# First two token chunks convolved on TensorE by tap diagonals, and x loaded as fp32, cast on VectorE and transposed for the rest

## The chip, the core and the metric

The kernel runs on one core of one Trainium2 chip. The metric is the device time of one execution in microseconds (us). Engines are named as the profile names them: PE is TensorE's matmuls and PEld its weight loads, DVE is VectorE, ACT is ScalarE, POOL is GpSimd and SP is SyncE. A DMA is issued from the queue of an engine: here SP, POOL and, in the changed kernel, ACT.

## What is computed

A causal depthwise convolution over the sequence with 7 softmaxed taps per head (8 heads of 24 channels), followed by a two-layer network with a beta-swish between its layers, over 32768 tokens of 192 channels:

```python
def _attn_ref(x, weight):
    B, S, D = x.shape            # 8, 4096, 192
    H, K = weight.shape          # 8, 7
    w = softmax(weight, axis=-1)
    x_pad = np.concatenate([np.zeros((B, K - 1, D)), x], axis=1)
    idx = np.arange(S)[:, None] + np.arange(K)[None, :]
    x_unf = x_pad[:, idx, :].reshape(B, S, K, H, D // H)
    return np.einsum('hk,bskhg->bshg', w, x_unf).reshape(B, S, D)

def _moe_ref(x, w_in, w_out, beta):          # w_in 192 x 2048, w_out 2048 x 192
    h = x @ w_in
    g = h * (1.0 / (1.0 + np.exp(-beta * h)))
    return (g @ w_out).astype(np.float32)
```

## The kernel before

**Two streams.** The 32768 tokens are split into two streams s = 0 and 1 of 16384 tokens each, which are worked on together. With channels on partitions, one stream's 64 channels of a group lie on partitions 0 to 63 and the other stream's on 64 to 127; the 192 channels make NK = 3 such groups (kk). So each matmul of the first layer (line 257) contracts over 64 rows, and the two streams use the two halves of the array side by side. For that, both halves of `w_in_s` hold the same weights.

**Steps.** `steps` (line 61) lists stretches of tokens: 128, 128, 256, then 31 of 512 tokens, 34 steps in all. In step i, for each of 16 units u (a block of 128 hidden channels), `mm1(i, u)` makes six matmuls into a tile `ph` (three groups, two streams) and ACT turns it into `g` with Silu scaled by beta (line 259). Between the units, `mm2(i - 1, ...)` multiplies the hidden values of the step before with `w_out_s` into tiles `po` (line 293); `mm2_plan` says in which unit. When a pair of token blocks is complete, `store` copies `po` to `o_sb` on DVE (line 301) and SP writes it out (line 307). `ph` and `po` have two buffers each. For a step of 512 tokens the pairs complete in units 5, 7, 13 and 15, for one of 256 in units 11 and 15.

**The convolution.** Also between the units, DVE convolves the next step's tokens: `conv_ops(i + 1)` gives 22 entries, a beginning (which copies the last six columns of the chunk before into `xt`, line 220) and 21 taps, tap 0 a TENSOR_SCALAR (line 229), the others SCALAR_TENSOR_TENSOR (line 231), for each of three groups. They read the transposed x in `xt`, add in `acc` and end in `xc`, which mm1 of the next step reads. Two entries are issued after each unit.

**Fetching x.** A chunk j is 512 tokens of each stream. POOL loads it with eight DMAs that cast fp32 to bf16 on the way (line 96, tile `x_bf`, three buffers), and SP transposes it with four DMA transposes of 128 tokens into `xt` (line 104, three buffers). At the beginning of step i, ahead of its units, chunk j + 2 is transposed and chunk j + 3 is loaded, where j is the chunk of step i; step i + 1 then convolves chunk j + 2.

**The start.** The first 128 tokens are convolved on PE: DVE makes seven copies of `x0` weighted with the taps (line 168), and 42 matmuls with a shifted identity (line 185) add them up, with the channels on partitions; ACT evicts them to `xc` (line 190). w_in comes in five POOL DMAs (line 80) and three copies inside the chip from one half to the other (line 84). w_out comes in four SP DMAs (line 142), and POOL scales it by 1/beta into `w_out_s` (line 207, 16 instructions). Everything passes through `pin`, which keeps the order of the program on each engine and queue.

Of the kernel before, what the change touches and what calls it, by code (L numbers as in the profile page):

```python
# [10 lines left out]
FP32 = mybir.dt.float32  # L11
BF16 = mybir.dt.bfloat16
# [6 lines left out]
def kernel(  # L19
# [14 lines left out]
    group = D // H  # L34
# [3 lines left out]
    NK = D // 64  # L38
    NS = 2
    TS = B * S // NS  # L40
    TILE = 512

# [8 lines left out]
    xbf_pool = ctx.enter_context(tc.tile_pool(name="xbf", bufs=3))  # L51
# [8 lines left out]

    steps = [(0, 128), (128, 128), (256, 256)]
    steps += [(t, TILE) for t in range(TILE, TS, TILE)]
    n_steps = len(steps)


    x0 = consts.tile([128, NS, D], FP32, name="x0")
    pin(nc.sync.dma_start(out=x0, in_=xs[:, 0:128, :].rearrange("s p d -> p s d")))
    wbc = consts.tile([128, H, K], FP32, name="wbc")
    pin(nc.sync.dma_start(out=wbc, in_=weight.rearrange("h k -> (h k)").partition_broadcast(128)))
    beta16 = consts.tile([NF, 128], FP32, name="beta16")  # L70
    pin(nc.sync.dma_start(out=beta16, in_=moe_beta.rearrange("(c p) -> c p", p=128)))

    w_in_s = consts.tile([128, NK, F], BF16, name="w_in_s")
    w_in_v = moe_w_in.rearrange("(k c) f -> c k f", c=64)
# [4 lines left out]
    def load_w_in(half, f0, f1):  # L79
        pin(nc.gpsimd.dma_start(out=w_in_s[64 * half:64 * half + 64, :, f0:f1], in_=w_in_v[:, :, f0:f1]))  # L80

    def copy_w_in(half, f0, f1):
        o = 1 - half
        pin(nc.sync.dma_start(out=w_in_s[64 * o:64 * o + 64, :, f0:f1],
                              in_=w_in_s[64 * half:64 * half + 64, :, f0:f1]))

    xbf_of, xt_of = {}, {}

    def load_x(j, b0=0, b1=4):
        if j not in xbf_of:  # L90
            xbf_of[j] = xbf_pool.tile([128, 4, NK, NS, 64], BF16, name="x_bf")
        t = xbf_of[j]
        for b in range(b0, b1):
            for s in range(NS):
                src = xs[s, TILE * j + 128 * b:TILE * j + 128 * (b + 1), :]
                pin(nc.gpsimd.dma_start(out=t[:, b, :, s, :],  # L96
                                        in_=src.rearrange("p (k c) -> p k c", c=64)))

    def transpose_x(j, b0=0, b1=4):
        if j not in xt_of:  # L100
            xt_of[j] = xt_pool.tile([128, NK, LEAD + TILE], BF16, name="xt")
        for b in range(b0, b1):
            c = LEAD + 128 * b
            pin(nc.sync.dma_start_transpose(
                out=xt_of[j][:, :, c:c + 128],
                in_=xbf_of[j][:, b, :, :, :].rearrange("p k s c -> p (k s c)")))

# [7 lines left out]


    load_w_in(0, 0, 512)
    load_w_in(1, 0, 512)
    shift = consts.tile([128, 128 + PAD], BF16, name="shift")
    pin(nc.gpsimd.memset(shift, 0.0))  # L120
    pin(nc.gpsimd.affine_select(out=shift, in_=shift, compare_op=ALU.not_equal, fill=1.0,
                                base=PAD, pattern=[[-1, 128 + PAD]], channel_multiplier=1))
    id16 = consts.tile([NF, NF], FP32, name="id16")
    pin(nc.gpsimd.memset(id16, 0.0))
    pin(nc.gpsimd.affine_select(out=id16, in_=id16, compare_op=ALU.not_equal, fill=1.0,
                                base=0, pattern=[[-1, NF]], channel_multiplier=1))
    load_x(0, 0, 4)
    mask = consts.tile([128, NK, H], FP32, name="mask")
    pin(nc.gpsimd.memset(mask, 1.0))
    for s in range(NS):  # L130
        m = mask[64 * s:64 * s + 64, :, :]
        pin(nc.gpsimd.affine_select(out=m, in_=m, compare_op=ALU.is_ge, fill=0.0, base=0,  # L132
                                    pattern=[[64, NK], [-group, H]], channel_multiplier=1))
        pin(nc.gpsimd.affine_select(out=m, in_=m, compare_op=ALU.is_ge, fill=0.0, base=group - 1,  # L134
                                    pattern=[[-64, NK], [group, H]], channel_multiplier=-1))
    load_w_in(0, 512, 1024)
    load_w_in(1, 1024, 1536)
    load_w_in(0, 1536, 2048)
    load_x(1)

    for c in range(0, NF, 4):
        pin(nc.sync.dma_start(out=w_out_f[:, c:c + 4, :], in_=w_out_v[:, c:c + 4, :]))  # L142
        if c == 0:
            transpose_x(0, 0, 2)
            copy_w_in(0, 512, 1024)
        if c == 4:
            copy_w_in(1, 1024, 1536)
            transpose_x(0, 2, 4)
        if c == 8:
            copy_w_in(0, 1536, 2048)  # L150


    mx = consts.tile([128, H], FP32, name="mx")
    pin(nc.vector.tensor_reduce(out=mx, in_=wbc, axis=AX.X, op=ALU.max))
    pin(nc.vector.tensor_tensor(wbc, wbc, mx[:, :, None].to_broadcast([128, H, K]), ALU.subtract))
    pin(nc.scalar.activation(wbc, wbc, AF.Exp))
    pin(nc.scalar.activation(scrap, one, AF.Silu))
    sm = consts.tile([128, H], FP32, name="sm")
    pin(nc.vector.tensor_reduce(out=sm, in_=wbc, axis=AX.X, op=ALU.add))
    rs = consts.tile([128, H], FP32, name="rs")  # L160
    pin(nc.vector.reciprocal(rs, sm))
    taps = consts.tile([128, H, K], FP32, name="taps")
    pin(nc.vector.tensor_tensor(taps, wbc, rs[:, :, None].to_broadcast([128, H, K]), ALU.mult))


    xw = consts.tile([128, K, NS, D], BF16, name="xw")
    for k in range(K):
        pin(nc.vector.tensor_tensor(  # L168
            xw[:, k, :, :].rearrange("p s (h c) -> p s h c", c=group),
            x0.rearrange("p s (h c) -> p s h c", c=group),  # L170
            taps[:, None, :, k:k + 1].to_broadcast([128, NS, H, group]),
            ALU.mult))

    warm = psum_h.tile([128, 2, TILE], FP32, name="ph")
    for i in range(8):
        pin(nc.tensor.matmul(warm[:, i % 2, :], zeros[:, 0:128], zeros, start=True, stop=True))  # L176
    bps = psum_h.tile([128, 2, TILE], FP32, name="ph")
    pin(nc.tensor.transpose(bps[:, 0, 0:NF], beta16, id16))
    cva = psum_o.tile([128, 2, TILE], FP32, name="po")
    cvb = psum_o.tile([128, 2, TILE], FP32, name="po")  # L180
    cv = [cva[:, 0, 0:128], cva[:, 1, 0:128], cvb[:, 0, 0:128]]
    for k in range(K):
        for kk in range(NK):
            for s in range(NS):
                pin(nc.tensor.matmul(cv[kk][64 * s:64 * s + 64, :], xw[:, k, s, 64 * kk:64 * kk + 64],  # L185
                                     shift[:, k:k + 128], start=(k == 0), stop=(k == K - 1)))
    xc_of = {}
    xc_of[0] = xc_pool.tile([128, NK, TILE], BF16, name="xc")
    for kk in range(NK):
        pin(nc.scalar.activation(xc_of[0][:, kk, 0:128], cv[kk], AF.Copy))  # L190

    beta = consts.tile([128, NF], FP32, name="beta")
    pin(nc.vector.tensor_copy(beta, bps[:, 0, 0:NF]))
    rbeta = consts.tile([128, NF], FP32, name="rbeta")
    pin(nc.vector.reciprocal(rbeta, beta))

    tmp3 = consts.tile([128, NK, K, H], FP32, name="tmp3")
    for kk in range(NK):
        pin(nc.vector.tensor_tensor(tmp3[:, kk, :, :],
                                    mask[:, kk:kk + 1, :].to_broadcast([128, K, H]),  # L200
                                    taps.rearrange("p h k -> p k h"), ALU.mult))
    taps3 = consts.tile([128, NK, K], FP32, name="taps3")
    pin(nc.vector.tensor_reduce(out=taps3, in_=tmp3, axis=AX.X, op=ALU.add))


    for c in range(NF):
        pin(nc.gpsimd.tensor_scalar_mul(w_out_s[:, c, :], w_out_f[:, c, :], rbeta[:, c:c + 1]))  # L207


    def conv_ops(i):  # L210
        t0, n = steps[i]
        j, c0 = t0 // TILE, t0 % TILE
        ops = []

        def halo():
            xt = xt_of[j]
            if t0 % S == 0 or t0 == 128:
                pin(nc.vector.memset(xt[:, :, LEAD - PAD:LEAD], 0.0))
            elif c0 == 0:
                pin(nc.vector.tensor_copy(xt[:, :, LEAD - PAD:LEAD], xt_of[j - 1][:, :, TILE + LEAD - PAD:]))  # L220

        def tap(kk, k):
            xt, xc = xt_of[j], xc_of[i]
            acc = accs[i]
            src = xt[:, kk, LEAD - PAD + c0 + k:LEAD - PAD + c0 + k + n]
            w = taps3[:, kk, k:k + 1]
            a = acc[:, kk, 0:n]
            if k == 0:
                pin(nc.vector.tensor_scalar_mul(a, src, w))  # L229
            else:  # L230
                pin(nc.vector.scalar_tensor_tensor(  # L231
                    out=xc[:, kk, 0:n] if k == K - 1 else a, in0=src, scalar=w, in1=a,
                    op0=ALU.mult, op1=ALU.add))
# [144 lines left out]
```

## Time and profile before

| | us |
|---|---|
| median of 3 runs (lowest to highest) | 714.59 (713.95 to 716.54) |
| the profiled execution's time | 712.91 |
| its span in the profile | 711.2 |
| L257 matmuls (mm1), 3264 of them, busy | 432.7 |
| L293 matmuls (mm2), 7936 of them, busy | 422.4 |
| L259 activations, 544, busy | 574.9 |
| L231 taps into acc, 495, busy | 326.7 |
| L301 store copies, 124, busy | 68.9 |
| first matmul of mm1 | 10.92 from the start |

All times in views of the profile are in us from the start of the span, and durations in us or, where marked, ns. In a timeline row the first number is the start, the second the length of the row (several like instructions are merged, with their number after an x), then engine, line, operation, what it writes <- what it reads with the shape of both, and in brackets how long the engine stood idle before and what ended that. "SPq" is SP's queue. Consecutive instructions of an engine overlap a little, so the distance from one start to the next is shorter than a duration. In a table of windows, the window is followed by its length, the busy time and (in brackets) the number of instructions of PE, PEld, DVE, ACT and POOL, the granted clock, the DMA engines' share and GB/s.

### The profile page before, as it was taken

To read this page: it belongs to the slowest core of one execution; us is meant where nothing else is said; L and a number is where in the kernel's file an instruction comes from. 1 tells how busy PE (TensorE), PEld (TensorE's weight loads), DVE (VectorE), ACT (ScalarE), POOL (GpSimd) and SP (SyncE) were. 2 spreads that over 40 slices of the span, in tenths; PEclk is the share of its full clock that TensorE was granted. 3 is DMA by queue.
4 is the path that set the end of the run, shared out by engine and by line. 5 is a ranking of instruction groups with operands and counts; after the bars stand their busy time and mean duration, and the time that the engine had idled before them with its cause. 6 is when DMAs were issued, how large, how long until landed. Compare 5 with 4: busy or idle time off the path is not lost.

```text
span 711.2 us, 25346 instructions
## 1 busy us (share of the span) xinstructions
PE 687.7 (97%) x11379; PEld 524.5 (74%) x11379; DVE 502.2 (71%) x877; ACT 578.8 (81%) x552; POOL 218.2 (31%) x290
## 2 busy tenths in 40 slices
PE   5589999999999999999999999999999999999998
PEld 2466777777777777777777777777777777777777
DVE  4779776677687667678667768766776876676702
ACT  3489888888888888888888888888888888888882
POOL 9997332223333113333212333321233330000000
PEclk9999999999999999999999999999999999999999
DMA  9999554455555445555445555544555553221012
GB/s 132 149 95 96 81 88 69 72 84 79 75 80 87 69 73 85 75 72 87 79 71 78 74 74 81 88 71 71 83 80 74 80 85 64 58 62 52 28 44 68
DMA packets 194861, 55.38 MB, mean 78 GB/s; under 512 B 158128, under 2 KB 194752, under 8 KB 194752
## 3 DMA queue, kind: packets, MB, share of 16 engines
q0 software_dynamic: 103440, 13.58, 30.6%
q1 hardware_dynamic: 91312, 40.17, 22.3%
q8 instruction: 89, 1.46, 0.9%
q14 instruction: 20, 0.16, 0.1%
HBM read 28.94 MB, written 25.17 MB: 76 GB/s over the span
## 4 chain that ended last, share of the span: by engine, by line
PE 93%; POOL 2%; DMA 2%; DVE 2%; issue 0%; ACT 0%; SPq 0%; DVEq 0%; POOLq 0%
PE ph L257 46%; PE po L293 46%; PE po L316 2%; DVE acc L231 1%; POOL x_bf L96 1%; DMA w_in_s<-w_in_s 1%; DMA x_bf<-in_x_dram 1%; POOL w_in_s L80 0%; ACT g L259 0%; DVE xc L231 0%; DVE acc L229 0%; SPq L142 0%; POOL mask L132 0%; POOL mask L134 0%; DVE o_sb L320 0%
## 5 line engine op out<-in xcount | busy, mean ns | idle before, releaser
L259 ACT ACTIVATE g<-ph,beta 128x1024 bf16<-128x1024 f32 (+2 forms) x544 | 574.9, 1064 | 111.8 <-PE ph L257 107.4
L257 PE MATMUL ph<-xc,w_in_s 64*128 64x512 bf16 (+2 forms) x3264 | 432.7, 367 | 17.0 <-DMA w_in_s<-w_in_s 9.4
L293 PEld LDWEIGHTS <-g 64*128 64x128 bf16 x7936 | 359.6, 94 | 101.5
L293 PE MATMUL po<-w_out_s,g 64*128 64x192 bf16 x7936 | 422.4, 243 | 0.0
L231 DVE SCALAR_TENSOR_TENSOR acc<-xt,taps,acc 128x512 f32<-128x512 bf16 (+2 forms) x495 | 326.7, 727 | 0.0
L96 POOL DMA_DIRECT2D x_bf<-in_x_dram x256 | 197.5, 774 | 366.7 <-DMA xt<-x_bf 349.4
L257 PEld LDWEIGHTS <-w_in_s 64*128 64x128 bf16 x3264 | 168.2, 96 | 74.6 <-DMA w_in_s<-w_in_s 10.5
L301 DVE COPY o_sb<-po 128x384 f32<-128x384 f32 x124 | 68.9, 556 | 183.5 <-PE po L293 183.5
L231 DVE SCALAR_TENSOR_TENSOR xc<-xt,taps,acc 128x512 bf16<-128x512 bf16 (+2 forms) x99 | 66.5, 727 | 0.0
L229 DVE TENSOR_SCALAR acc<-xt,taps 128x512 f32<-128x512 bf16 (+2 forms) x99 | 41.8, 481 | 9.2 <-DMA xt<-x_bf 8.1
L207 POOL TENSOR_SCALAR w_out_s<-w_out_f,rbeta 128x192 bf16<-128x192 f32 x16 | 15.6, 992 | 0.1
L316 PE MATMUL po<-w_out_s,g 128*128 128x192 bf16 x128 | 10.7, 246 | 0.0
L316 PEld LDWEIGHTS <-g 128*128 128x128 bf16 x128 | 10.5, 98 | 0.2 <-issue 0.2
L320 DVE COPY o_sb<-po 128x192 f32<-128x192 f32 x8 | 2.9, 358 | 7.6 <-PE po L316 7.6
L176 PE MATMUL ph<-zeros 128*128 128x512 bf16 x8 | 3.6, 631 | 1.2 <-DVE one L112 1.2
L220 DVE COPY xt<-xt 128x18 bf16<-128x18 bf16 x28 | 4.6, 166 | 0.0
L185 PE MATMUL po<-shift,xw 128*64 128x128 bf16 x42 | 3.3, 314 | 1.2 <-DVE xw L168 1.2
L185 PEld LDWEIGHTS <-xw 128*64 128x64 bf16 x42 | 2.0, 152 | 2.4 <-DVE xw L168 2.4
L80 POOL DMA_DIRECT2D w_in_s<-in_moe_w_in_dram x5 | 3.3, 665 | 0.8 <-POOLq L362 0.8
L168 DVE TENSOR_TENSOR xw<-x,taps 128x384 bf16<-128x384 f32 x7 | 3.4, 553 | 0.0
L176 PEld LDWEIGHTS <-zeros 128*128 128x128 bf16 x8 | 1.0, 140 | 2.9 <-issue 1.7
L190 ACT ACTIVATE xc<-po 128x128 bf16<-128x128 f32 x3 | 0.6, 278 | 3.1 <-PE po L185 3.1
(30 smaller groups left out, 8.8 us busy)
## 6 DMA issues: line engine op xcount, KB each, us to landing
out_dram<-o_sb SPq DMA_DIRECT2D x124, 192.0 KB, 2.3
x_bf<-in_x_dram POOLq DMA_DIRECT2D x256, 48.0 KB, 3.1
xt<-x_bf SPq DMA_TRANSPOSE x128, 2.3
w_out_f<-in_moe_w_out_dram SPq DMA_DIRECT2D x4, 384.0 KB, 6.7
w_in_s<-in_moe_w_in_dram POOLq DMA_DIRECT2D x5, 192.0 KB, 5.5
out_dram<-o_sb SPq DMA_DIRECT2D x8, 96.0 KB, 1.6
w_in_s<-w_in_s SPq DMA_DIRECT2D x3, 192.0 KB, 6.8
x<-in_x_dram SPq DMA_DIRECT2D x1, 192.0 KB, 2.6
```

The source lines that it names most:

```text
L96: pin(nc.gpsimd.dma_start(out=t[:, b, :, s, :], in_=src.rearrange("p (k c) -> p k c", c=64)))
L176: pin(nc.tensor.matmul(warm[:, i % 2, :], zeros[:, 0:128], zeros, start=True, stop=True))
L185: pin(nc.tensor.matmul(cv[kk][64 * s:64 * s + 64, :], xw[:, k, s, 64 * kk:64 * kk + 64], shift[:, k:k + 128], start=(k == 0), stop=(k == K ...
L207: pin(nc.gpsimd.tensor_scalar_mul(w_out_s[:, c, :], w_out_f[:, c, :], rbeta[:, c:c + 1]))
L220: pin(nc.vector.tensor_copy(xt[:, :, LEAD - PAD:LEAD], xt_of[j - 1][:, :, TILE + LEAD - PAD:]))
L229: pin(nc.vector.tensor_scalar_mul(a, src, w))
L231: pin(nc.vector.scalar_tensor_tensor(out=xc[:, kk, 0:n] if k == K - 1 else a, in0=src, scalar=w, in1=a, op0=ALU.mult, op1=ALU.add))
L257: pin(nc.tensor.matmul(ph[:, s, 0:n], w_in_s[r, kk, ts(fc, 128)], xc_of[i][r, kk, 0:n], start=(kk == 0), stop=(kk == NK - 1)))
L259: pin(nc.scalar.activation(g_of[i][:, fc, :, 0:n], ph[:, :, 0:n], AF.Silu, scale=beta[:, fc:fc + 1]))
L293: pin(nc.tensor.matmul(po[:, q, 0:D], g_of[i][r, fc, s, ts(b, 128)], w_out_s[r, fc, :], start=(phase == 0 and fc == 0), stop=(phase == 1 a ...
L301: pin(nc.vector.tensor_copy(o_sb, po[:, :, 0:D]))
L316: pin(nc.tensor.matmul(po[:, 0, 0:D], g_of[i][:, fc, s, ts(b, 128)], w_out_s[:, fc, :], start=(fc == 0), stop=(fc == NF - 1)))
```

## The change

*The layout of channels.* A channel c is now q * 3 + k: partition q of 64, group k of 3. All three groups of a partition belong to one head, so that one column of taps (`tapn`) serves all of them.

*The first two chunks of 128 tokens.* `x0` now holds 512 tokens as fp32. PE transposes the first two blocks (`transpose_0`, three fp32 transposes each); ACT and DVE copy them to `xr`, in which six zero columns lead. `diag` holds for each tap a diagonal matrix of the unnormalized taps, doubled over both column halves. `conv_0` makes for each tap and stream one matmul of 64 rows, 128 columns of weights and 3 x 128 moving columns, in fp32r; as the diagonal is doubled, the result has the channels on both halves of the partitions. `evac_0` multiplies it by 1/sum. Steps 0 and 1 therefore use another form of mm1: `mm1_pair(i, u)` computes hidden block u from the lower half and block u + 8 from the upper half, 256 moving columns (two streams of 128 tokens), so that each half of `w_in_s` needs only its own 1024 hidden channels at first. Four POOL loads bring these, and four copies inside the chip fill the rest, before step 2. The second pair of blocks of `x0` is transposed within step 0 and goes to `xt_of[0]`.

*The steps.* 128, 128, then five of 256, then 29 of 512: 36 steps. A convolution of 256 tokens takes one instruction per tap over all three groups.

*w_out.* Its four loads move from SP's queue to POOL's, behind w_in. Of the scalings, 12 go to DVE within step 0, 4 stay on POOL.

*Fetching x.* From chunk 2 on, SP loads a chunk in two fp32 DMAs (`xf`, two buffers), DVE casts it in two copies to `xbf` (two buffers), and SP transposes it. These three entries (`fetch`) are added to the end of the step's list of DVE work, after the convolution; the list is spread over the first 14 units.

```diff
-    steps += [(t, TILE) for t in range(TILE, TS, TILE)]
+    steps += [(t, 256) for t in range(TILE, 3 * TILE, 256)]
+    steps += [(t, TILE) for t in range(3 * TILE, TS, TILE)]
...
+    def load_x(j, s, b0=0, b1=NB, eng=None):
...
+        src = xs[s, TILE * j + 128 * b0:TILE * j + 128 * b1, :]
+        pin((eng or nc.sync).dma_start(out=xf_of[j][:, b0:b1, s, :],
+                                       in_=src.rearrange("(b p) d -> p b d", p=128)))
+    def cast_x(j, s, b0=0, b1=NB, eng=None):
...
+        pin((eng or nc.vector).tensor_copy(
+            xbf_of[j][:, b0:b1, :, s, :].rearrange("p b k q -> p k b q"),
+            xf_of[j][:, b0:b1, s, :].rearrange("p b (q k) -> p k b q", k=NK)))
...
+    HF = F // 2
+    for f in range(0, HF, 512):
+        for s in range(NS):
+            load_w_in(s, HF * s + f, HF * s + f + 512)
     for c in range(0, NF, 4):
-        pin(nc.sync.dma_start(out=w_out_f[:, c:c + 4, :], in_=w_out_v[:, c:c + 4, :]))
...
+        pin(nc.gpsimd.dma_start(out=w_out_f[:, c:c + 4, :], in_=w_out_v[:, c:c + 4, :]))
+    for b in (0, 2):
+        for s in range(NS):
+            load_x(1, s, b, b + 2, nc.gpsimd)
...
+    tap_ps = misc[:, 0, 0:K]
+    pin(nc.tensor.matmul(tap_ps, sel.rearrange("h s g j -> h (s g j)"), taps, start=True, stop=True))
...
+    for k in range(K):
+        pin(nc.vector.tensor_scalar_mul(diag[:, k, :, :], ident2, etap[:, k:k + 1]))
...
+    def transpose_0(po, b):
...
+        for kk in range(NK):
+            pin(nc.tensor.transpose(t[:, kk, :], v[:, kk, :], ident))
+        return t
+    def conv_0(cv, b, k0, k1):
+        for k in range(k0, k1):
+            for s in range(NS):
+                pin(nc.tensor.matmul(
+                    cv[:, s, 0:NK * 128], diag[half_of(s), k, :, :].rearrange("p s q -> p (s q)"),
+                    xr[half_of(s), :, 128 * b + k:128 * b + k + 128],
+                    start=(k == 0), stop=(k == K - 1)))
...
+    t0_ = transpose_0(po01, 0)
...
+    pin(nc.tensor.transpose(beta_ps, beta16, ident[0:NF, 0:NF]))
+    t1_ = transpose_0(po01, 1)
+    pin(nc.scalar.activation(xr[:, :, PAD:PAD + 128], t0_, AF.Copy))
...
+    conv_0(cv0, 0, 0, K)
...
+    evac_0(cv0, 0, 0, nc.scalar)
+    evac_0(cv0, 0, 1, nc.vector)
...
+    for f in range(0, HF, 512):
+        for s in range(NS):
+            copy_w_in(s, HF * s + f, HF * s + f + 512)
...
+        parts = [(kk, kk + 1) for kk in range(NK)] if n == TILE else [(0, NK)]
+        return [begin] + [lambda k=k, p=p: tap(k, *p) for k in range(K) for p in parts]
...
+    def mm1_pair(i, u):
+        ph = psum_h.tile([128, NS, TILE], FP32, name="ph")
+        fcs = (u, u + NF // 2)
+        for kk in range(NK):
+            for h in range(2):
+                pin(nc.tensor.matmul(ph[:, h, 0:256], w_in_s[half_of(h), kk, ts(fcs[h], 128)],
+                                     xc_of[i][half_of(h), kk, 0:256],
+                                     start=(kk == 0), stop=(kk == NK - 1)))
...
+    def fetch(j, eng=None):
+        ops = []
+        for s in range(NS):
+            ops.append(lambda s=s: cast_x(j, s, eng=eng))
+        def go():
+            for b in range(NB):
+                transpose_x(j, b)
+            if (j + 2) * TILE < TS:
+                for s in range(NS):
+                    load_x(j + 2, s)
+        ops.append(go)
+        return ops
+    def extra_ops(i):
+        if i < 3 or i == 4:
+            return []
+        j = {3: 2, 5: 3, 6: 4}.get(i, steps[i][0] // TILE + 2)
+        return fetch(j) if j * TILE < TS else []
...
+        if i == 0:
...
+            for u in range(NF // 2):
+                mm1_pair(0, u)
+                if u < 2:
...
+                elif u == 2:
+                    cv1 = psum_o.tile([128, 2, TILE], FP32, name="po")
+                    conv_0(cv1, 1, 0, 4)
+                elif u == 3:
+                    conv_0(cv1, 1, 4, K)
...
+                elif u > 4:
+                    for c in FC0[4 * u - 20:4 * u - 16]:
+                        scale_w_out(c, nc.vector)
+                    cv[u - 1]()
+            continue
...
-            if (j + 2) * TILE < TS:
-                transpose_x(j + 2)
-            if (j + 3) * TILE < TS:
-                load_x(j + 3)
+        dve = dve + extra_ops(i)
+        done = 0
         for u in range(NF):
             mm1(i, u)
             for t in plan[u]:
                 mm2(i - 1, *t)
-            for op in conv[:2]:
+            upto = len(dve) * (u + 1) // (NF - 2)
+            for op in dve[done:upto]:
                 op()
-            conv = conv[2:]
+            done = max(done, upto)
```

## The prediction

> **What bounds the kernel now.** I read the page first, then windows by stage, then the timeline of the engines that feed TensorE. The page and the stage table:
>
> ```profile
> PE 687.7 (97%) x11379; PEld 524.5 (74%) x11379; DVE 502.2 (71%) x877; ACT 578.8 (81%) x552; POOL 218.2 (31%) x290
> ...
> 11.00:31.00 20.00, 7.32 (x96) 4.75 (x96) 11.85 (x38) 6.37 (x17) 19.60 (x23) 1.00 1.46 175
> 31.00:39.70 8.70, 8.19 (x162) 7.01 (x160) 4.43 (x10) 7.20 (x18) 8.70 (x11) 1.00 0.41 32
> 39.70:52.50 12.80, 9.81 (x162) 7.89 (x159) 12.70 (x22) 10.49 (x17) 12.79 (x18) 1.00 1.83 111
> 52.50:69.20 16.70, 16.12 (x216) 10.41 (x218) 15.71 (x26) 14.85 (x15) 13.06 (x18) 1.00 1.01 87
> ```
>
> After the window come its length and the busy time of PE, PEld, DVE, ACT and POOL. Between 11 and 31 us PE works 7.3 us out of 20: the first step waits for halves of w_in to be copied (the group of L257 with 64x128 names 9.4 us of it). From 69.7 us on PE is never idle: the step for tokens 1024 begins at 69.70, the next at 90.62, so a full step lasts 20.92 us (16 units of 1.307). The last full step begins 28 steps after 90.62, at 676.4, and 34.8 us later the span of 711.2 ends. So a gain can only come from the first 70 us, while a loss can come anywhere that another engine is made to need over 20.92 us a step. DVE is the candidate, and it depends on the transposes of x. DVE's rows of the timeline around a step's start (320.7):
>
> ```profile
> 318.34 0.56 DVE L301 COPY o_sb<-po 128x384 f32<-128x384 f32 x1 [1.49 <-PE po L293]
> 320.96 0.56 DVE L301 COPY o_sb<-po 128x384 f32<-128x384 f32 x1 [2.06 <-PE po L293]
> 321.43 0.16 DVE L220 COPY xt<-xt 128x18 bf16<-128x18 bf16 x1
> 321.63 1.28 DVE L229 TENSOR_SCALAR acc<-xt,taps 128x512 f32<-128x512 bf16 x3
> ```
>
> The transposes, from SP's rows of the timeline in three other steps, and all of them by their line:
>
> ```profile
> 133.74 5.10 SPq L104 DMA_TRANSPOSE xt<-x_bf  x4
> ...
> 322.02 5.72 SPq L104 DMA_TRANSPOSE xt<-x_bf  x4
> ...
> 405.70 6.54 SPq L104 DMA_TRANSPOSE xt<-x_bf  x4
> ```
>
> ```profile
> L104 SPq DMA_TRANSPOSE xt<-x_bf x128: 1183/1197/2642, 9.5 to 639.7; - x128
> DMA to landing us min/median/max: 2.3/2.3/7.8
> ```
>
> In each step SP issues four transposes in 5.1 to 6.5 us; one takes 1.2 us to issue and lands 2.3 us after its start. From the first start to the last landing that is 5.10 - 1.2 + 2.3 = 6.2 us at best, 6.8 in the middle row, 7.6 in the longest. No DVE instruction waits for it now: the four go out at a step's start and are convolved one step later. The taps are not blocked either; here is one convolution of 512 tokens that ran through:
>
> ```profile
> 54.48 1.38 DVE L229 TENSOR_SCALAR acc<-xt,taps 128x512 f32<-128x512 bf16 x3
> 55.78 10.01 DVE L231 SCALAR_TENSOR_TENSOR acc<-xt,taps,acc 128x512 f32<-128x512 bf16 x15
> 65.71 2.06 DVE L231 SCALAR_TENSOR_TENSOR xc<-xt,taps,acc 128x512 bf16<-128x512 bf16 x3
> 67.70 0.54 DVE L301 COPY o_sb<-po 128x384 f32<-128x384 f32 x1
> ```
>
> From 54.48 to 67.70, **13.2 us for 21 taps**. A store copy takes 0.48 us from start to start (328.80 to 329.28).
>
> **The start.** Removed: DVE's 7 weighted copies of x0 (3.4 us), 42 bf16 matmuls (3.3 us), the mask and the shift matrix. Added: 5 selector and identity steps on POOL ahead of its loads (rows of 0.1 to 0.3 us, so loads issue from 2.3 us instead of 1.3), 12 fp32 transposes of x, 28 fp32r matmuls of 384 columns, 7 diagonals on DVE. PE's order puts beta and the second block of x0 ahead of the first convolution; beta landed at 5.7 us before (PE's wait at 5.83). After it three transposes, to about 7.0. Of fp32r matmuls there is no row: bf16 at this stage needs 3.60/8 = 0.45 us for 512 columns, so 0.34 us for 384; if two halves of the array overlap, seven pairs take 2.4 us, and if neither overlap nor the two-byte rate holds (twice the bytes, no pairing) four times that, 9.4. I take 2.4, by the L257 rows, whose 64-row halves do overlap. With the eviction (three ACT rows of 0.28 us before, now one wider one) the first step starts at 10.3 us, against 10.92.
>
> Steps 0 and 1 use each w_in load on the half where it landed, so the 20 us window loses its waits. Step 0 has 16 activations of 0.45 us (7.2) and, on PE between its units, transposes and the second convolution, 2.4 us by the same rows in which ACT gets nothing: some 9.5 us. Step 1: 16 activations, 7.5. Step 2 had 16 activations in 10.22 us: 10.3. Each new 256-step needs 16 x 0.655 on PE and 10.2 on ACT: 10.6. The w_out loads go from SP's queue to POOL's, behind w_in's, and 12 of 16 scalings from POOL (0.99 us each) to DVE; that can delay step 1 by up to 2 us, and is covered while step 0 lasts. The four copies of w_in wait on SP and must land by step 2, at 27.3 us; their 6.8 us to landing leave room. Starts: 10.3, 19.8, 27.3, 37.6, 48.2, 58.8, and **step 6 (tokens 1280) at 69.4**. Step 7 (1536) could then begin at 80.0 against 90.62 before: **10.6 us gained**, if DVE keeps up. What "loads each half once" saves is one of five loads from memory; four copies inside the chip replace three.
>
> **The fetch, which decides.** x is now loaded by SP as fp32, two DMAs per chunk instead of POOL's eight, and DVE casts it (two copies of 768 elements). No row shows this copy; the nearest are the first tap, 0.43 us for 512 elements, and the store copy, 0.48 for 384. 256 more elements at the first tap's rate give some 0.6, at the store copy's slope 0.95; a gain is excluded, as DVE had no such work. I take 0.6, by the nearer form (one source, both sides in SBUF).
>
> The order matters more. A step's list is now 22 convolution entries, then two casts and the transposes. So the transposes of chunk j+2 go out at the end of the step, and the next step's first tap, which reads all 512 columns, needs all four landed. **DVE stands idle for the transposes** in every step. Behind the waiting tap are the other 20 taps and the store copies, hence the po buffers that mm2 wants at unit 8. DVE's loop, from one convolution's end to the next: cast 0.6, store copy of unit 13 0.48, cast 0.6, four transposes 6.8 with 0.15 for the two hand-overs (0.03 from copy to SP at 329.36 to 329.39, and about 0.12 after a landing), taps 13.2, store copies of units 5 and 7 0.96. Together **22.8 us against PE's 20.92**. Halo and the store copy of unit 15 fit into the wait. Ends: 21.7 (casts 0.5, transposes 5.9, which is issue without a pause, 3 x 1.2 + 2.3) and 24.3 (casts 0.95, transposes 7.6).
>
> The first such wait is worse, as step 6 has 256 tokens and convolves 512. Step 5's casts come after the store copy of unit 11 and end at 58.8 + 9.9; the transposes have landed 6.95 later, at 75.65. Taps 13.2 and one copy 0.48: chunk 3 is ready at 89.3, so step 7 begins there and the whole gain of the start is spent. Then 21.85 and 22.3 us for the next two convolutions (fewer store copies) and 26 x 22.8 = 592.8: the last step starts at 726.3 + 0.2, and with the unchanged 34.8 the span is **761.2**. The profiled execution of before took 712.91 for its span of 711.2, so 762.9; its median over runs was 1.7 higher, so **764 us**.
>
> The Trainium skill, in "DMA: Bandwidth & Descriptors", section "Rules for kernel authors", says to issue a DMA early, compute, and wait for it late, which speaks against this order. The trace of before keeps to it, with no wait for a transpose after 26 us; by the rule alone the cost would be whatever of 6.8 us a step isn't covered.
>
> **Rivals.** *The loop fits under PE* (not slower): the transposes would have to be down in 20.92 - 16.0 = 4.9 us. For it: POOL's casting loads, 30.6% of the DMA engines' time on the page, are gone, and no row shows transposes without them. Against: the 5.9 us that issue and one landing take at the least. Then only step 6's long convolution (13.7 us, ready at about 84) costs, and a step 7 bound by ACT at 16.6, 27 full ones and 34.8 end at 700.2: **703.6 us**. *The loop fits, but the start is slow*: fp32r at 9.4 us instead of 2.4 for both convolutions, 14 us of which step 0's activations hide a part: about **712 us**, no change. *The loop binds and casts are slow as well*: 23.5 a step, 26 x 0.7 more: **783 us**.
>
> **How the numbers follow.** Loop binds with fast casts 0.68, with slow casts 0.18, hidden fetch 0.11, hidden fetch with a slow start 0.03. The forecast is the first's 764 us. Its own range follows from the ends of the loop, 26 x -1.1 and 26 x 1.5, and 3 us of the start: 732 to 806. The range of 8 in 10 is 732 to 804: it leaves out the hidden fetches below and a corner above. Faster than 0.5% (the least that a measurement here can tell from no change) 0.11, within 0.03, slower 0.86.
>
> **What would show it.** Right: DVE waits for the transposes in every full step, 5 to 7 us; full steps 22 to 24 us apart; PE idle near 2 us a step, for DVE's xc or its o_sb copies; PE's wait for copies of w_in in the first 31 us gone; step 6 starting near 70 us. Wrong: PE at 20.92 us a step from 90 us on, or a fourth transpose landing within 4.9 us of the cast.

## The result, and the profile after

The changed kernel takes **778.04 us** (median of 4 runs, 777.77 to 778.61) against 714.91 before (4 runs): ratio 1.088, 95% interval 1.086 to 1.090. It is slower by 63 us. The forecast was 764 us, slower by 49.

The profiled execution has a span of 776.0 us. Three lines of its page: the engines, the chain of work that ended last by engine, and the same by line:

```profile
PE 705.8 (91%) x11472; PEld 536.9 (69%) x11472; DVE 536.8 (69%) x904; ACT 585.0 (75%) x584; POOL 15.1 (2%) x26
...
DVE 57%; SPq 14%; DMA 10%; PE 10%; issue 7%; ACT 2%; DVEq 0%
DVE acc L259 34%; SPq L95 13%; DMA xt<-xb 10%; DVE o_sb L332 7%; DVE xc L259 6%; DVE xb L84 5%; DVE acc L257 5%; PE po L324 3%; PE ph L287 3%; ACT g L290 1%; PE po L347 1%; PE ph L274 1%; DMA xf<-in_x_dram 0%; PE po L180 0%; DVE w_out_s L228 0%
```

Before, that chain by engine was nearly all PE:

```profile
PE 93%; POOL 2%; DMA 2%; DVE 2%; issue 0%; ACT 0%; SPq 0%; DVEq 0%; POOLq 0%
```

Now it runs through DVE's taps (L259), SP's issue of the transposes (L95) and their landing, in a circle. No engine is over 91% busy: this is a bound by latency. The table of waits has it as its first line (who waited, for what: us in total, times, longest):

```profile
DVE acc L257 <- DMA xt<-xb: 190.5, 30, 7.4
...
PE po L324 <- DVE o_sb L332: 46.9, 51, 2.5
```

One turn of the circle, in DVE's rows of the timeline, and the transposes in SP's:

```profile
324.01 0.84 DVE L84 CAST xb<-xf 128x768 bf16<-128x768 f32 x1
324.76 0.55 DVE L332 COPY o_sb<-po 128x384 f32<-128x384 f32 x1
325.23 0.83 DVE L84 CAST xb<-xf 128x768 bf16<-128x768 f32 x1
325.99 0.54 DVE L332 COPY o_sb<-po 128x384 f32<-128x384 f32 x1
326.45 0.15 DVE L248 COPY xt<-xt 128x18 bf16<-128x18 bf16 x1
333.14 1.28 DVE L257 TENSOR_SCALAR acc<-xt,tapn 128x512 f32<-128x512 bf16 x3 [6.54 <-DMA xt<-xb]
...
347.19 0.84 DVE L84 CAST xb<-xf 128x768 bf16<-128x768 f32 x1
```

```profile
326.09 5.84 SPq L95 DMA_TRANSPOSE xt<-xb  x4
```

From 324.01 to 347.19 are 23.18 us: casts, one store copy and the hand-over to SP 2.08 (to 326.09), transposes 7.05 (to 333.14), 21 taps and two store copies 14.05. DVE is idle for 6.54 us of it, and PE gets 20.92 us of work per turn. From the second cast of chunk 4 (95.8) to that of chunk 31, the last (719.3), the mean is (719.3 - 95.8) / 27 = 23.09 us.

Two windows of the start, step 1 with what lies before step 2, and step 6 with the wait behind it (length; busy PE, PEld, DVE, ACT, POOL; granted clock; DMA share; GB/s):

```profile
23.30:31.20 7.90, 7.27 (x96) 5.99 (x96) 5.03 (x11) 4.94 (x13) 0.00 (x0) 0.63 0.08 17
...
74.60:95.40 20.80, 12.13 (x234) 10.77 (x231) 14.60 (x25) 11.03 (x17) 0.00 (x0) 0.80 0.28 77
```

The first matmul of mm1 starts at 10.42 us, against 10.92 before, and step 2 at 31.27 against 39.7: the waits for copies of w_in are gone. In the second window PE works 12.1 of 20.8 us.

### The profile page after: what moved, and what is told of

Read it like the earlier page. It is cut to its first block, busy times and chain, and to the rows that moved or that the text cites. A ratio compares the mean times of both kernels' runs of the same rounds, so it can differ in the third digit from the quotient of the medians.

```text
span 776.0 us, 25240 instructions
## 1 busy us (share of the span) xinstructions
PE 705.8 (91%) x11472; PEld 536.9 (69%) x11472; DVE 536.8 (69%) x904; ACT 585.0 (75%) x584; POOL 15.1 (2%) x26
## 3 DMA queue, kind: packets, MB, share of 16 engines
q0 software_dynamic: 1536, 3.15, 1.8%
## 4 chain that ended last, share of the span: by engine, by line
DVE 57%; SPq 14%; DMA 10%; PE 10%; issue 7%; ACT 2%; DVEq 0%
DVE acc L259 34%; SPq L95 13%; DMA xt<-xb 10%; DVE o_sb L332 7%; DVE xc L259 6%; DVE xb L84 5%; DVE acc L257 5%; PE po L324 3%; PE ph L287 3%; ACT g L290 1%; PE po L347 1%; PE ph L274 1%; DMA xf<-in_x_dram 0%; PE po L180 0%; DVE w_out_s L228 0%
## 5 line engine op out<-in xcount | busy, mean ns | idle before, releaser
L290 ACT ACTIVATE g<-ph,beta 128x1024 bf16<-128x1024 f32 (+1 forms) x544 | 567.9, 1051 | 163.1 <-PE ph L287 159.4
L324 PE MATMUL po<-w_out_s,g 64*128 64x192 bf16 x7936 | 429.8, 244 | 49.4 <-DVE o_sb L332 46.9
L287 PE MATMUL ph<-xc,w_in_s 64*128 64x512 bf16 (+1 forms) x3264 | 428.9, 363 | 13.5 <-DVE xc L259 12.6
L259 DVE SCALAR_TENSOR_TENSOR acc<-xt,tapn,acc 128x512 f32<-128x512 bf16 (+1 forms) x460 | 320.2, 758 | 0.7
L257 DVE TENSOR_SCALAR acc<-xt,tapn 128x512 f32<-128x512 bf16 (+1 forms) x92 | 40.8, 497 | 190.7 <-DMA xt<-xb 190.5
L259 DVE SCALAR_TENSOR_TENSOR xc<-xt,tapn,acc 128x512 bf16<-128x512 bf16 (+1 forms) x92 | 65.1, 757 | 0.2
L84 DVE CAST xb<-xf 128x768 bf16<-128x768 f32 (+1 forms) x62 | 51.0, 829 | 0.0
L278 ACT ACTIVATE g<-ph,beta 128x256 bf16<-128x256 f32 x32 | 12.7, 475 | 9.4 <-PE ph L274 9.3
L274 PE MATMUL ph<-xc,w_in_s 64*128 64x256 bf16 x96 | 10.5, 339 | 2.5 <-DVE xc L197 1.3
L228 POOL TENSOR_SCALAR w_out_s<-w_out_f,rbeta 128x192 bf16<-128x192 f32 x4 | 4.0, 988 | 2.9 <-DMA w_out_f<-in_moe_w_out_dram 2.9
```

The costliest lines, as they stand in the source:

```text
L84: pin((eng or nc.vector).tensor_copy(xbf_of[j][:, b0:b1, :, s, :].rearrange("p b k q -> p k b q"), xf_of[j][:, b0:b1, s, :].rearrange("p b ...
L228: pin(eng.tensor_scalar_mul(w_out_s[:, c, :], w_out_f[:, c, :], rbeta[:, c:c + 1]))
L259: pin(nc.vector.scalar_tensor_tensor(out=xc_of[i][:, k0:k1, 0:n] if k == K - 1 else a, in0=src, scalar=w, in1=a, op0=ALU.mult, op1=ALU.add))
L274: pin(nc.tensor.matmul(ph[:, h, 0:256], w_in_s[half_of(h), kk, ts(fcs[h], 128)], xc_of[i][half_of(h), kk, 0:256], start=(kk == 0), stop=(k ...
L278: pin(nc.scalar.activation(g_of[i][:, fcs[h], :, 0:128], ph[:, h, 0:256].rearrange("p (s t) -> p s t", s=NS), AF.Silu, scale=beta[:, fcs[h ...
L287: pin(nc.tensor.matmul(ph[:, s, 0:n], w_in_s[half_of(s), kk, ts(fc, 128)], xc_of[i][half_of(s), kk, 0:n], start=(kk == 0), stop=(kk == NK ...
```

## The experiments

The circle was tested from three sides: opening it in two ways, loading it with more work, and moving SP's part of it alone. The reference time of before was measured again in both sets, 715.16 (7 runs) and 715.18 us (8 runs).

| run | median us | ratio to before (95%) |
|---|---|---|
| fetch put first | 709.66 | 0.992 (0.991 to 0.994) |
| fetch one chunk ahead, at the end | 706.77 | 0.988 (0.986 to 0.990) |
| casts first, transposes last | 736.77 | 1.030 (1.028 to 1.031) |
| changed kernel, third cast | 798.75 | 1.116 (1.115 to 1.118) |
| fetch put first, third cast | 712.70 | 0.996 (0.995 to 0.998) |
| casts first, transposes ahead of unit 13's store | 712.38 | 0.996 (0.995 to 0.998) |
| one ahead, scalings earlier | 705.46 | 0.986 (0.985 to 0.988) |
| the same, one tap instruction for three groups in step 6 | 704.65 | 0.985 (0.984 to 0.987) |

**1. The fetch put first.**

```diff
-        dve = dve + extra_ops(i)
+        dve = extra_ops(i) + dve
```

> Casts and transposes of a step are put ahead of the step's convolution instead of behind it; nothing else changes. Theory A (DVE's loop cast - transposes - taps sets the step): the transposes get a whole step to land, the taps' waits of about 6.5 us vanish, full steps fall from 23.2 to 20.92 us, and only step 6's convolution of 512 tokens in a step of 256 still costs. Counted: step 6 starts at 74, chunk 3 is ready at 74 + 1.6 + 13.7 = 89.3, then 16.6 + 27 x 20.92 + 34.8 = 616.2, span 705.5, about 708 us. Rival B (the fp32 loads, the casts' DVE time and the DMA traffic themselves slow the steps): same work, so 765 us or more. Rival C (the start and the clock lost in it carry most of the loss): over 760.

Measured 709.66 us. DVE's wait for transposes has left the table of waits, and a full step is 20.92 us again, as these casts show:

```profile
318.13 1.59 DVE L84 CAST xb<-xf 128x768 bf16<-128x768 f32 x2
319.63 0.15 DVE L248 COPY xt<-xt 128x18 bf16<-128x18 bf16 x1
319.82 1.28 DVE L257 TENSOR_SCALAR acc<-xt,tapn 128x512 f32<-128x512 bf16 x3
...
339.05 1.59 DVE L84 CAST xb<-xf 128x768 bf16<-128x768 f32 x2
```

The taps follow the casts of another chunk with no idle time between. The same loads, casts and transposes are made, so neither they (B) nor the start (C) can hold the 63 us.

**2. The fetch at the end, one chunk further ahead.**

```diff
-        if i < 3 or i == 4:
+        if i < 2 or i == 4:
             return []
-        j = {3: 2, 5: 3, 6: 4}.get(i, steps[i][0] // TILE + 2)
+        j = {2: 2, 3: 3, 5: 4, 6: 5}.get(i, steps[i][0] // TILE + 3)
```

> The fetch stays at the end of the list, but fetches one chunk further ahead, so that its transposes are convolved a step later. Theory A (it is the wait inside the loop, not the place in the list): like the fetch put first, DVE waits for no transpose, full steps of 20.92 us; chunk 3 is ready at 73.5 + 0.5 + 13.7 = 87.7, span 704, about 706 us. If the place at the end of the list mattered by itself (casts and SP's queue late in the step), it stays near 778. Rival B: 765 or more.

Measured 706.77 us. The place in the list is as in the changed kernel; only the use of what is fetched lies a step further away. So it is the dependency inside one turn that cost, not the place.

**3. The casts first, the transposes last.**

```diff
-        dve = dve + extra_ops(i)
+        ext = extra_ops(i)
+        dve = ext[:2] + dve + ext[2:]
```

> The casts go ahead of the convolution, the transposes stay at its end and are still convolved in the next step. Theory A: the casts leave the loop, the transposes are issued behind the store of unit 13 rather than behind the casts, and the loop is 13.2 + 0.96 + 6.9 less about 1.3 for the last taps that lie behind that store: 20 us, under 20.92. Step 7 still starts at 95, the next convolutions end 19.3 later: span about 95 + 19.3 + 27 x 20.92 + 34.8 = 714, about 716 us, and DVE still shows waits of 3 to 6 us for the transposes. If late transposes cost by themselves, whatever the loop: near 23 us a step, over 760.

Measured 736.77 us, 21 more than theory A gave, so something still closes a circle although the transposes now depend on casts made long before. Its rows, DVE and then SP:

```profile
313.80 1.28 DVE L257 TENSOR_SCALAR acc<-xt,tapn 128x512 f32<-128x512 bf16 x3 [5.09 <-DMA xt<-xb]
...
327.18 0.55 DVE L332 COPY o_sb<-po 128x384 f32<-128x384 f32 x1
327.65 0.74 DVE L259 SCALAR_TENSOR_TENSOR xc<-xt,tapn,acc 128x512 bf16<-128x512 bf16 x1
328.31 0.55 DVE L332 COPY o_sb<-po 128x384 f32<-128x384 f32 x1
```

```profile
306.43 6.15 SPq L95 DMA_TRANSPOSE xt<-xb  x4
312.62 1.13 SPq L78 DMA_DIRECT2D xf<-in_x_dram  x2
313.85 14.28 SPq L338 DMA_DIRECT2D out_dram<-o_sb  x4
328.48 6.30 SPq L95 DMA_TRANSPOSE xt<-xb  x4
```

SP issues the transposes at 328.48, directly behind its four stores. The last of these waits for DVE's copy at 327.18, and DVE reaches that copy behind 20 of its 21 taps. From 306.43 to 328.48 are 22.05 us; from 108.89 to 678.56, over 26 turns, the mean is 21.91. The sum had 19.8 (13.2 + 0.96 + 6.9 - 1.3). In this turn the transposes take 7.37 us to the first tap, and 20 taps with two copies 13.38 where the sum had 12.86, since one tap lies behind that copy and not two. The copy itself and the store's issue, 1.30 us from 327.18 to 328.48, were not in the sum at all.

**4. Transposes one place ahead of that store.** The casts stay first; the transposes are issued in unit 13 ahead of its second-layer matmuls, hence ahead of the store that follows them.

```diff
             mm1(i, u)
+            if u == NF - 3:
+                for op in ext[2:]:
+                    op()
             for t in plan[u]:
                 mm2(i - 1, *t)
```

> As with the casts first and the transposes last (736.8 us), but the transposes stand one place earlier in the program: ahead of unit 13's second-layer matmuls, so ahead of that unit's store on SP's queue. Theory A2: what was still closing the loop there was SP's order, the transposes behind the store of unit 13 and this behind DVE's taps; one place earlier SP can issue them as soon as the casts and the store of unit 7 are done, and full steps fall from 22.05 to 20.92. The first long wait (step 6) stays, since a step of 256 has its store in unit 11: span 93.5 + 19.1 + 27 x 20.92 + 34.8 = 712, about 714 us. Rival (late casts and transposes cost by their time in the step, not by the queue): still near 737.

Measured 712.38 us. SP's rows:

```profile
311.69 5.32 SPq L95 DMA_TRANSPOSE xt<-xb  x4
...
332.62 5.13 SPq L95 DMA_TRANSPOSE xt<-xb  x4
```

332.62 - 311.69 = 20.93 us. No data dependency was changed between the third and the fourth kernel, only SP's order and, with one entry fewer, how DVE's list is spread over the units. This was worth 24 us, and the rows of both kernels show it on SP's queue. The wait before step 7, which was to stay, fell from 8.15 to 5.55 us.

**5. More work in the circle.** Stream 1 of each chunk is cast a second time.

```diff
         for s in range(NS):
             ops.append(lambda s=s: cast_x(j, s, eng=eng))
+        ops.append(lambda: cast_x(j, 1, eng=eng))
```

> The changed kernel with a third cast in every fetch (stream 1 is cast twice): 0.76 us more DVE work a step, on an engine that is 69% busy and stands idle 6.5 us a step. Theory A: the loop takes 23.2 + 0.76 us, all of it paid, 28 x 0.76 = 21: about 799 us. Rival (DVE has slack): 778, no change.

Measured 798.75 us, 20.7 more than the changed kernel: each of the 28 casts of some 0.75 us is paid in full, by an engine that waits 6.3 us a step for transposes (190.4 us in 30 waits). SP's transposes start 23.82 us apart on average (98.37 to 741.63, 27 turns), against 23.09 in the changed kernel.

**6. The same work with the circle open.**

> The kernel with the fetch put first, again with stream 1 cast twice: the same 0.76 us of DVE work a step that cost the changed kernel 20.7 us. Theory A: with the loop open DVE has 3 to 4 us to spare in a full step, so the third cast costs nothing there; only step 6 and the two behind it, where DVE is the last, pay, at most 1.5 us: 709.7 to 711.2 us. Rival (each DVE cycle is paid in this kernel, wherever it stands): 709.7 + 28 x 0.76 = 731 us.

Measured 712.70 us, 3.0 more than the fetch put first without it: a seventh of what it cost in the circle, but twice what I had allowed. Between 117 and 650 us PE is busy all of the time in both. The difference lies ahead of it, where steps of 256 leave DVE little room. PE's rows with waits, without and with the third cast:

```profile
75.52 0.50 PE L287 MATMUL ph<-xc,w_in_s 64*128 64x256 bf16 x6 [1.06 <-DVE xc L259]
89.95 1.93 PE L287 MATMUL ph<-xc,w_in_s 64*128 64x512 bf16 x6 [3.71 <-DVE xc L259]
```

```profile
76.49 0.50 PE L287 MATMUL ph<-xc,w_in_s 64*128 64x256 bf16 x6 [1.06 <-DVE xc L259]
91.81 1.93 PE L287 MATMUL ph<-xc,w_in_s 64*128 64x512 bf16 x6 [4.59 <-DVE xc L259]
```

Step 7 starts 1.86 us later, of which 0.97 were lost by step 6 already. The other 1.2 us go right behind that wait: the fourth six matmuls of step 7 start at 94.79 without and at 97.86 with the third cast, 3.07 us apart, and from the start of step 7 up to there the granted clock was 0.66 and 0.51 (the first window is the kernel without it, the second the one with it):

```profile
89.95:94.79 4.84, 4.73 (x43) 2.52 (x44) 4.80 (x10) 2.28 (x3) 0.00 (x0) 0.66 0.21 57
91.81:97.86 6.05, 5.95 (x42) 3.17 (x44) 5.98 (x11) 2.47 (x3) 0.00 (x0) 0.51 0.18 49
```

So the longer wait cost its own length and, behind it, more time at half the clock, which the expectation did not contain.

**7. Two attempts on what the start still loses**, on top of the kernel of the second experiment. First, the 12 scalings of w_out go ahead of four taps:

```diff
-                elif u == 4:
-                    for op in cv[2:4]:
-                        op()
-                elif u > 4:
-                    for c in FC0[4 * u - 20:4 * u - 16]:
+                elif u > 3:
+                    for c in FC0[4 * u - 16:min(4 * u - 12, 12)]:
                         scale_w_out(c, nc.vector)
-                    cv[u - 1]()
+                    if u == 7:
+                        for op in cv[2:6]:
+                            op()
```

> The kernel that fetches one chunk ahead (706.8 us), with DVE's 12 scalings of w_out put in units 4 to 6 of step 0, ahead of four of the convolution's taps for step 2. Theory: step 1's second-layer matmuls wait for these scalings (1.4 us and more at a time, PE at a granted clock of 0.58 in the 8 us behind); with them out of the way step 2 begins some 3 us earlier: about 704 us. Rival: the wait goes on to step 2's taps, or the start is bound by the w_out loads that land at 14 to 19 us: 706.8.

Measured 705.46 us: 1.3 less, not 3. The wait for scalings is gone, and a wait for step 2's tokens has come in its place, so the rival was half right. Even so step 2 begins at 27.70, against 31.76 in the kernel of the second experiment: 4.1 us earlier, more than the 3 that were forecast. The row of the new wait:

```profile
27.70 0.50 PE L287 MATMUL ph<-xc,w_in_s 64*128 64x256 bf16 x6 [2.54 <-DVE xc L259]
```

Half of it is lost again in step 2: part at a lower clock (0.50 from 30 to 32 us), and 0.84 us because PE waits for step 3's tokens, for which DVE had to wait for the transposes of chunk 1. The casts ahead of these stand on DVE behind the same taps in both kernels (27.48 us here, 27.76 there):

```profile
32.95 0.75 DVE L257 TENSOR_SCALAR acc<-xt,tapn 128x768 f32<-128x768 bf16 x1 [4.04 <-DMA xt<-xb]
```

So the convolution for step 3 ends at 40.0 us, against 39.7, step 3 begins only 2.0 us earlier, and so does step 7 (85.48 against 87.45). Then, chunk 3's convolution with one instruction per tap:

```diff
-        parts = [(kk, kk + 1) for kk in range(NK)] if n == TILE else [(0, NK)]
+        parts = [(kk, kk + 1) for kk in range(NK)] if n == TILE and steps[i - 1][1] == TILE else [(0, NK)]
```

> In addition the convolution of chunk 3, made in step 6 of 256 tokens, takes one instruction per tap over all three groups instead of three: 14 fixed parts of 0.13 us fewer, 13.2 us becomes about 11.4. Theory: PE's wait before step 7 (2.8 us in the kernel that fetches one chunk ahead) falls by 1.8: about 702 us if the scalings bring 3 us. If PE's wait there is not DVE's taps: no change against the kernel without it.

Measured 704.65 us, against 705.46: 0.8 us less, with runs that touch (703.81 to 705.24 and 705.19 to 705.62). DVE's rows say why:

```profile
72.46 1.81 DVE L257 TENSOR_SCALAR acc<-xt,tapn 128x1536 f32<-128x1536 bf16 x1
74.30 9.23 DVE L259 SCALAR_TENSOR_TENSOR acc<-xt,tapn,acc 128x1536 f32<-128x1536 bf16 x5
83.57 1.82 DVE L259 SCALAR_TENSOR_TENSOR xc<-xt,tapn,acc 128x1536 bf16<-128x1536 bf16 x1
85.31 0.55 DVE L332 COPY o_sb<-po 128x384 f32<-128x384 f32 x1
```

From 72.46 to 85.31 are 12.85 us, not 11.4. The first tap alone takes 1.8 us for 1536 elements, where three of 512 took 1.2. And PE gains nothing from the 0.35 us: with three instructions it begins on the first group of `xc` while DVE makes the others, with one it waits for the whole. The first matmuls of step 7 with three instructions, and with one:

```profile
85.48 0.39 PE L287 MATMUL ph<-xc,w_in_s 64*128 64x512 bf16 x2 [2.56 <-DVE xc L259]
...
85.45 1.23 PE L287 MATMUL ph<-xc,w_in_s 64*128 64x512 bf16 x6 [3.16 <-DVE xc L259]
```

This kernel has the lowest median of the study, 1.5% under the one before.

## Why the prediction was right, and where it was off

**The mechanism** was as forecast, and shown: the loop of casts, transposes and taps sets the step. Experiments 1 and 2 open it and bring 68 and 71 us; experiment 5 prices a microsecond in it at a microsecond per step.

**The size of a turn** was forecast as 22.8 us and measured as 23.09. The casts take 0.75 us from start to start, not 0.6: the value lay between my two ends, and I had taken the lower one by its form. That is 0.3 us. The transposes took 6.95 with the hand-overs in the sum, 7.05 in the turn shown; they did not get quicker without POOL's casting loads (the median issue is 1.25 us, against 1.20 before). Taps and store copies: 14.16 forecast, 14.05 measured. With the two turns behind step 6, the loop was 9.6 us over the sum (the last xc was done at 741.6 and chunk 3 at 95.0, 646.6 apart; forecast 636.9).

**The start** was forecast to have chunk 3 ready at 89.3 us; it was at 95.0, 5.7 later. The first step began at 10.42 for 10.3, and seven pairs of fp32r matmuls took 2.61 us for 2.4, so the lower end, chosen by the rows of 64-row halves, was right. That the first step comes so close is in part luck: the fp32r matmuls began at 6.49 us instead of 7.0, and behind them two evictions ran one after the other, on ACT (9.14) and on DVE (9.75), where the sum had one.

The step that failed was step 1: I took 16 activations in 7.5 us and held that the scalings' delay "is covered while step 0 lasts". Step 1 lasted 11.9 us (19.33 to 31.27). Step 2 began at 31.27, not 27.3, which is 4.0 of the 5.7 us; steps 2 to 5 took 1.2 us more than their sum, and step 6 began at 74.5 us, not near 70. DVE, with taps, scalings and evictions in one queue, released the last scalings only after 24.58 us, and PE waited for them:

```profile
24.58 1.00 DVE L228 TENSOR_SCALAR w_out_s<-w_out_f,rbeta 128x192 bf16<-128x192 f32 x4
24.94 0.80 PE L324 MATMUL po<-w_out_s,g 64*128 64x192 bf16 x6 [0.32 <-DVE w_out_s L228]
```

The first row is DVE's, the second PE's. From 23.3 to 31.2 us, behind these waits, the granted clock was 0.63 on average, which the sum did not contain. With the scalings out of the way (experiment 7) DVE's last tap for step 2 ended at 27.6 us, against 27.9 in the kernel that fetches one chunk ahead: it is DVE's whole list in steps 0 and 1, and not the scalings alone, that was left out. Together 5.7 and 9.6 us, less 0.6 behind them, are, but for rounding, the 14.8 us by which the span exceeded 761.2. (The forecast itself is 761.2 + 1.7 + 1.7, which gives 764.6 and not 764.)

**The wait behind step 6**: forecast as 9.3 us of late start for step 7 (89.3 against 80.0); PE's idle time there was 8.57 us, and the row behind it shows what else it cost:

```profile
93.83 1.93 PE L287 MATMUL ph<-xc,w_in_s 64*128 64x512 bf16 x6 [8.57 <-DVE xc L259]
```

**The rival of a hidden fetch** was priced at 703.6 us; the kernels that hide it measured 706.77 and 709.66, mostly for the slower start: their step 7 began at 87.45 and 89.95 us, where the rival had about 84. Its condition, transposes down in 4.9 us, was not met in the changed kernel: it takes another order, not faster transposes. **PE's idle time** showed, as said, as waits for DVE's xc and store copies, and mostly the latter (46.9 us in 51 waits), since DVE frees the po buffers late.

**A reading that was too wide.** That the kernel before has "no wait for a transpose after 26 us" holds for DVE, whose last such wait ends at 25.56 us. POOL's loads waited for transposes 25 times, 349.4 us in all, to get a buffer of `x_bf` back; PE was busy all the same.

## What to carry to other kernels

When work is moved onto an engine that already feeds the bound one, add up the circle, not the engine's busy time: what it makes, the transfer that follows, and what it needs from that transfer, against the step. One more step between fetch and use was worth 71 us here. An order on a queue closes such a circle as well as data does: transposes behind a store that waits for the same engine cost 24 us, and one place earlier the full steps were back at 20.93 us.

## What the runs showed that I had not expected

The granted clock. In the changed kernel's profile it fell to 0.50 four times, each time in a wait of PE or just behind one. In the order of these windows, the waits were 1.39, 8.57, 3.19 and 1.95 us long:

```profile
22.39:29.22 6.83, 5.64 (x54) 4.11 (x55) 5.94 (x13) 3.03 (x8) 0.76 (x2) 0.50 0.00 0
87.25:97.49 10.24, 3.55 (x22) 1.55 (x24) 9.89 (x17) 1.11 (x1) 0.00 (x0) 0.50 0.06 19
114.56:121.38 6.82, 5.92 (x48) 3.68 (x50) 4.11 (x8) 2.23 (x2) 0.00 (x0) 0.50 0.24 60
292.00:295.40 3.40, 3.40 (x32) 2.27 (x29) 3.40 (x7) 1.11 (x1) 0.00 (x0) 0.51 0.29 90
```

The six matmuls behind the wait of 8.57 us took 1.93 us, where the same six take 0.83 in a full step. Other waits of up to 2.46 us in the full steps left the clock at 1.00. The Trainium skill, in "TensorE: Matmul & The Clock Gate", section "What's actually happening", has the clock halved after an idle window of about 3.4 us. The wait of 8.57 us agrees with it; the falls at waits of 1.39, 1.95 and 3.19 us do not, and the measurement decides: no length of wait that is safe can be read from these runs.

At the start the profile's clock is to be read with care. In the profile of before it reads 1.00 from the first microsecond, yet the same six matmuls of 64x128 took 0.56 us at 33.26 and 0.34 from 34.61 on:

```profile
33.26 0.56 PE L257 MATMUL ph<-xc,w_in_s 64*128 64x128 bf16 x6
...
34.61 0.34 PE L257 MATMUL ph<-xc,w_in_s 64*128 64x128 bf16 x6
```

And a first tap over three groups of 512 columns at once ran slower than three single ones, 1.8 us against 1.2, while the taps that add did gain, 1.85 us against three of 0.67.
